# Fewer chunks of 384 tokens, more of 512, and three transforms packed more closely

## The chip, the cores and the metric

One core of one Trainium2 chip. The metric is the device time of one execution in microseconds (us), the median of several runs.

## The reference

The input x has 4 batches of 3008 positions with 256 channels. Per batch: a real Fourier transform along the positions, a complex 256x256 mix with biases, a soft threshold of 0.01 on real and imaginary parts, and the inverse transform. The 12032 resulting rows ("tokens") then go through a two-layer network with 2048 hidden units and a leaky activation whose slope is learned per unit:

```python
X = np.fft.rfft(x, axis=1); Xr, Xi = X.real, X.imag
Yr = Xr @ w_r - Xi @ w_i + b_r
Yi = Xr @ w_i + Xi @ w_r + b_i
Yr = np.sign(Yr) * np.maximum(np.abs(Yr) - lam, 0.0)      # Yi likewise
y = np.fft.irfft(Yr + 1j * Yi, n=x.shape[1], axis=1).reshape(-1, 256)
h = y @ w_in
out = (np.maximum(h, 0.0) + alpha * np.minimum(h, 0.0)) @ w_out
```

## The kernel before

**The transform** of a batch is four stages of matrix products, 3008 being 47 x 64. Stage a works on 16 row groups (`a_split`, `a_mm`, `a_evac`) and stores its result to a DRAM tile `ad`. Stage b reads that back in another order, in 12 pairs (`b_load`, `b_mm`, `b_evac`, `b_evac2`). On each pair the complex mix follows with three real products (`m_mm` two, `m_mm2` the third), the threshold in eight parts (`m_part`, lines 520 to 538), and stage c (`c_mm`, `c_evac`), stored to a DRAM tile `zd`. Stage d reads `zd` in 8 blocks of 376 tokens a batch; it is the "last stage" and yields tokens as columns, split into a high and a low float32r part (`d_load`, `d_mm`, `d_part`, `d_step`; in the wide part `s_dmm`, `s_dpart`). So in each batch all of a comes before the first pair of b, and all of c before the first block of d, through DRAM.

**The network, classic part.** Tokens 0 to T0 are cut into CC chunks of 384 (the first of a run of 16 has 256). One step is one chunk and one of 16 tiles of 128 hidden units. `l1_step` makes six matmuls of up to 384 columns into PSUM (three products of high and low parts, two halves of the channels), ACT takes the relu of the negated sum (line 686), DVE adds it scaled (687), ACT makes the high part gh (691), and DVE or POOL in turn the low part gl (692). `l2_step` makes nine matmuls of 256 columns for the step three behind. At the end of a chunk the third accumulator goes out through the tile `ot`, the other two through `os`.

**The network, wide part.** From T0 on, chunks of 512 tokens, in pairs of hidden tiles, PR = 8 pairs a chunk (`s_l1`, `s_sums`, `s_l2`): twelve matmuls of 512 columns, then seven block products in place of eight (21 matmuls of 256 columns instead of 24), with sums and differences of blocks on ACT, DVE and POOL. Pair 1 of each chunk takes the eight plain products. The last chunk has 384 tokens and is classic in its products. `s_out` and `s_turn` combine and transpose the result.

**The order** is written out by hand in program order; each engine and each DMA queue executes its instructions in that order and waits on semaphores. `at(i, fn, ...)` files work under classic step i. In a step, `l1_step` runs first, with the work of `mid` (parts of the mix) inside it; then the stores collected before are issued on SP's queue (`put`), then `l2_step`, then the work of `todo`. Batch 0 is transformed before the classic part begins. Of batch b + 1, row group g of stage a stands at step AO[b+1] + 3g/2 (its split two steps earlier, its load of x five steps before), and pair q at a step i: `b_load` at i - 4, `b_mm` to `b_evac2` at i, `m_mm` at i + 2, the mix's third product and parts at i + 3 to i + 6, `c_mm` and `c_evac` at i + 8. Batch 1's row groups are done by step 15. The first 48 steps run the first J = 3 chunks side by side, while the network's weights are taken apart (`pump`). Blocks of the last stage stand three steps ahead of their chunk (61, 77, 93, 109, ...). The 26 last classic steps prepare the weights of the wide part (`w_open`, `w_full`, `w_sums`, `w_split`), in the buffers of the transforms' tables, and its first blocks. In the wide part `pre` and `post` file the blocks of the last stage under pairs.

**Buffers that the change touches in time.** `ps_f` is a PSUM pool of three buffers for the outputs of stages a, b, the mix, c and d in program order; `ps_h` has two for L1. `ot` (line 722) and `sm`, the sum of stage b (line 453), share one buffer. `zst` (two buffers) holds the outputs of c and, in batches 2 and 3, of a, until their stores have landed. `xt` (two) holds loads of x, `bt` (three) those of stage b. `Xh` and `Xl` (two each) hold a pair from i to i + 4.

Of the kernel before, what the change touches and what calls it, by code (L numbers as in the profile page):

```python
# [93 lines left out]
def fft_mix_moe(ctx, tc, x, w_r, w_i, b_r, b_i, w_in, w_out, alpha, la, rb, lc, rd, lf, cf, sel, out):  # L94
# [12 lines left out]
    TC = 384  # L107
    assert NC * TC - 128 == NC * TOK

    CC = 16  # L110
    SC = 512

    def head(c):
        return 128 - (TC - TOK) * (c % NC) if c % NC else 0

    def size(c):
        return TC if c % NC else TC - 128

    T0 = (CC // NC) * NC * TOK + TC * (CC % NC) - (128 if CC % NC else 0)
    NS2 = -(-(B * S - T0) // SC)  # L120
# [12 lines left out]
    def f(t):  # L133
        return t.bitcast(F32)
# [443 lines left out]
    def d_open(c):  # L578
# [3 lines left out]
        if head(c):  # L582
            for t, src in zip((hi, lo), heads.pop(c)):
                if c < CC:
                    t, src = t[:, :, 0:head(c)], f(src)[:, :, 0:head(c)]
# [8 lines left out]
    def d_step(b, g):  # L594
        t = zt.pop((b, g))
        c = NCH * b + g
        assert c < CC
        n0 = (size(c) - head(c)) // CH
# [20 lines left out]
    def s_open(n):  # L619
        yt[CC + n] = [work.tile([128, CT, SC], F32R, tag=tag, name=tag) for tag in ("yh", "yl")]  # L620

    def s_parts(dg):

        s, e = TOK * dg, TOK * dg + TOK
        for n in range(max(s - T0, 0) // SC, (e - 1 - T0) // SC + 1):
            a, z = max(s, T0 + SC * n), min(e, T0 + SC * (n + 1))
            yield n, (a - s) // CH, (z - s) // CH, a - T0 - SC * n, z - T0 - SC * n
# [7 lines left out]
    def s_dpart(dg, n):  # L635
        parts = []
        for k, n0, n1, a, z in s_parts(dg):
            if k == n:
                for ct in range(CT):
                    ps = ds[dg][ct][:, :, n0:n1]  # L640
                    ys = [y[:, ct] for y in yt[CC + n]]
                    if n == NS2 - 1:
# [92 lines left out]
    PR = FT // 2  # L735
# [39 lines left out]
    def s_l1(n, t):  # L775
        yh, yl = yt[CC + n]
        w1 = SC if n < NS2 - 1 else ZC
        q = work.tile([128, 2, SC], F32, tag="xt", name="sq")[:, :, 0:w1]
        for j in range(2):
            m = 2 * t + j  # L780
            ps = ps_h.tile([128, SC], F32, tag="h", name="ps_h")[:, 0:w1]
            k = 0
            for ct in range(CT):
                for w, a in ((0, yh), (0, yl), (1, yh)):
                    PE.matmul(ps, wi_h[m // FH][:, w, ct, 128 * (m % FH):128 * (m % FH) + 128], a[:, ct, 0:w1],  # L785
                              start=(k == 0), stop=(k == 3 * CT - 1))
                    k += 1
            A.activation(out=q[:, j], in_=ps, func=AF.Relu, scale=-1.0)  # L788
            V.scalar_tensor_tensor(out=q[:, j], in0=q[:, j], scalar=beta_s[:, m:m + 1], in1=ps,  # L789
                                   op0=ALU.mult, op1=ALU.add)  # L790
        sq[n, t] = q
# [160 lines left out]
    ES = [1, 1, 1, 1, 1, 1, 1, 1, 1, 0, 1, 0, 0, 0, 0, 0]  # L952
    LOS = [0, 1, 0, 0, 1, 1, 0, 1, 1, 0, 1, 1, 0, 1, 0, 0, 1, 1, 0, 0, 1, 0, 1, 1, 1, 1, 1, 0, 1, 1, 0, 1, 1, 0, 1, 1, 0, 1, 1, 0, 1, 1, 0, 1, 1, 0, 1, 1]
    DS = 3
    AO = {2: 92, 3: 146}
    BO = {2: 126, 3: 176}
    BP = 4
    SLAG = 2
    PLAIN = (1,)
    MP = [3, 4, 4, 4, 4, 5, 5, 6]  # L960
    CM = 8
    PB = 49
    BL = 4
    LM = 26
    MM, M2 = 2, 4
# [17 lines left out]
    with tc.manual_schedule():  # L983
# [100 lines left out]
        def at(i, fn, *args, when=todo):  # L1084
            when.setdefault(i, []).append((fn, args))
# [9 lines left out]
        for b in range(B):  # L1095
            s0 = b * per
            for g in range(J if b == 0 else 0, min(NCH, CC - NCH * b)):
                i = s0 + g * FT
                at(i - 8, d_load, b, g)
                at(i - 4 if i == J * FT else i - FT + 1, d_open, NCH * b + g)  # L1100
                if b == 0 and g == J:
                    at(i - DS, d_step, b, g)
                else:
                    at(i - 3, d_step, b, g)
            if b == 0:
                for g in range(FILL, NG):
                    i = 6 * (g - FILL) + 9
                    if g % 2 == 0:
                        at(i - 8, a_load, 1, g // 2)
                    at(i, a_mm, 1, g)  # L1110
                    at(i, a_evac, 1, g)
            else:
                for g in range(NG if b + 1 < B else 0):
                    i = AO[b + 1] + 3 * g // 2
                    if g % 2 == 0:
                        at(i - 5, a_load, b + 1, g // 2)
                    at(i - 2, a_split, b + 1, g)
                    at(i, a_mm, b + 1, g)
                    at(i, a_evac, b + 1, g)
            for q in range(NPAIR if b + 1 < B else 0):  # L1120
                i = PB + 11 * q // 2 if b == 0 else BO[b + 1] + BP * q
                at(i - BL, b_load, b + 1, q)
                at(i, b_mm, b + 1, q)
                at(i, b_evac, b + 1, q)
                at(i, b_evac2, b + 1, q)
                at(i + MM, m_mm, b + 1, q)
                at(i + M2, m_mm2, b + 1, q, when=mid)
                for n, k in enumerate(MP):
                    at(i + k, m_part, b + 1, q, n, when=mid)
                at(i + MP[6], m_evac1, b + 1, q)  # L1130
                at(i + CM, c_mm, b + 1, q)
                at(i + CM, c_evac, b + 1, q)
# [3 lines left out]
        pre, post = {}, {}  # L1136
        i = NS - 26
        at(i, w_open)
        for p in range(PR // 2):
# [3 lines left out]
            for k in range(2):  # L1143
                at(i + 6 * p + 3 + k, w_split, p, k, False)
                at(i + 6 * p + 4 + k, w_split, p, k, True)
        at(NS - 14, d_open, CC)
        for dg in range(CC, B * NCH):
            ns = [n for n, *_ in s_parts(dg)]
            first = PR * (ns[-1] - 1) - 1
            if len(ns) == 2:  # L1150
                at(first, s_dmm, dg, when=pre)
                at(first, s_dpart, dg, ns[0], when=pre)
                at(first, s_open, ns[1], when=post)
                at(first, s_dpart, dg, ns[1], when=post)
            elif dg > CC:
                first += 6
                at(first, s_dmm, dg, when=pre)
                at(first, s_dpart, dg, ns[0], when=pre)
            else:
                first = -6  # L1160
                at(NS - 6, s_dmm, dg)
                at(NS - 6, s_dpart, dg, ns[0])
            if first < 0:
                at(NS + first - 5, d_load, dg // NCH, dg % NCH)
            else:
                at(first - 3, d_load, dg // NCH, dg % NCH, when=pre)
# [25 lines left out]
        for k in range(len(spairs) + SLAG):  # L1192
# [9 lines left out]
            if k >= SLAG:  # L1202
                n, t = spairs[k - SLAG]
# [43 lines left out]
```

## Time and profile before

| | us |
|---|---|
| runs, three | 1369.5, 1369.52, 1370.37; median 1369.52 |
| the profiled execution | 1370.45 |
| its span, first to last instruction | 1368.7 |

The profile's page gives, for each engine, its busy time and share of the span: PE is TensorE's matmuls, PEld its weight loads, DVE VectorE, ACT ScalarE, POOL GpSimd; SP is the engine that issues most DMAs.

| engine | busy share |
|---|---|
| PE | 99% |
| PEld | 93% |
| DVE | 73% |
| ACT | 55% |
| POOL | 29% |

A matmul's end is modelled and matmuls overlap, so its start, and the distance to the next start, say more than its duration. In the profile the first matmul of a classic step starts at 108.4 us, the first of the wide part at 836.5 us. A timeline row is: start, duration, engine, line, operation, output<-input, shapes, count, and in brackets the idle time of the engine ahead of it with what ended it.

### The profile page before, as it was taken

The page shows a single profiled execution, that of the slowest core. Times are in us where ns is not written, and L with a number is a line of the kernel's source. Part 1 is how long each engine was busy: PE and PEld are TensorE (multiplying, and loading weights), DVE is VectorE, ACT ScalarE, POOL GpSimd, SP SyncE. Part 2 cuts the span into 40 slices and gives each one's busy share as a digit, 9 for nine tenths or more (in the row PEclk, how much of TensorE's full clock was granted, in tenths as well). Part 3 has the DMA queues.
Part 4 walks back from the last instruction along what each step waited for, and adds up shares of the span by engine and source line. Part 5 has one row for each costly group of instructions (what it writes and reads, how often), then busy time and mean ns, then how long its engine had stood idle before and what let it go on. Part 6 is the DMA issues. An engine that isn't in the chain of part 4 may idle for free.

```text
span 1368.7 us, 25199 instructions
## 1 busy us (share of the span) xinstructions
PE 1352.7 (99%) x9367; PEld 1274.7 (93%) x9367; DVE 993.1 (73%) x1821; ACT 749.5 (55%) x1528; POOL 400.1 (29%) x421
## 2 busy tenths in 40 slices
PE   8999999999999999999999999999999999999998
PEld 5979899999999999899999999999999999999998
DVE  2767855666665677676777667788888888888885
ACT  3566555445565455554545555555565556555653
POOL 3864832222222322223323221211121211211222
PEclk9999999999999999999999999999999999999999
DMA  9965222113332124321211111010011101110001
GB/s 234 258 175 151 78 93 67 50 36 85 120 92 74 47 85 127 95 72 62 65 45 58 44 36 36 12 28 16 13 40 28 26 5 37 29 28 7 22 17 28
DMA packets 82903, 89.66 MB, mean 66 GB/s; under 512 B 35567, under 2 KB 65234, under 8 KB 82781
## 3 DMA queue, kind: packets, MB, share of 16 engines
q1 hardware_dynamic: 74214, 76.76, 19.4%
q0 software_dynamic: 5168, 8.02, 2.2%
q10 hardware_dynamic: 3399, 3.27, 0.7%
q8 instruction: 74, 1.21, 0.4%
q14 instruction: 48, 0.39, 0.1%
HBM read 50.49 MB, written 34.34 MB: 62 GB/s over the span
## 4 chain that ended last, share of the span: by engine, by line
PE 92%; DVE 3%; ACT 2%; issue 1%; DMA 1%; POOL 0%; ACTq 0%; SPq 0%; DVEq 0%; POOLq 0%
PE ps_h L785 19%; PE ps_h L680 17%; PE ps_m L486 5%; PE ps_o L887 4%; PE ps_o L888 4%; PE ps_o L886 4%; PE ps_o L719 4%; PE ps_o L718 4%; PE ps_o L717 4%; PE ps_d L611 4%; PE ps_b L426 3%; PE ps_m L473 3%; PE o_last L719 2%; PE o_last L717 2%; PE o_last L718 2%; PE ps_a L387 2%
## 5 line engine op out<-in xcount | busy, mean ns | idle before, releaser
L680 PE MATMUL ps_h<-yh,w 128*128 128x384 f32 (+1 forms) x960 | 282.8, 336 | 1.6 <-DVE q L687 1.5
L785 PE MATMUL ps_h<-yh,w 128*128 128x512 f32 (+1 forms) x768 | 251.7, 388 | 0.0
L687 DVE SCALAR_TENSOR_TENSOR q<-q,beta_s,ps_h 128x384 f32<-128x384 f32 (+1 forms) x256 | 154.5, 604 | 123.1 <-ACT q L686 122.0
L691 ACT ACTIVATE gh<-q 128x384 fp32r<-128x384 f32 (+1 forms) x256 | 132.8, 519 | 186.2 <-DVE q L687 181.9
L692 POOL TENSOR_TENSOR gl<-q,gh 128x384 fp32r<-128x384 f32 (+1 forms) x123 | 132.1, 1075 | 349.1 <-ACT gh L691 326.8
L824 POOL TENSOR_TENSOR l<-t,h 128x512 fp32r<-128x512 f32 x77 | 99.9, 1297 | 389.8 <-ACT h L822 357.6
L680 PEld LDWEIGHTS ps_h<-yh,w 128*128 128x128 f32 x960 | 176.7, 189 | 4.8 <-issue 1.3
L785 PEld LDWEIGHTS ps_h<-yh,w 128*128 128x128 f32 x768 | 143.9, 188 | 26.1
L789 DVE SCALAR_TENSOR_TENSOR sq<-sq,beta_s,ps_h 128x512 f32<-128x512 f32 (+1 forms) x192 | 133.9, 731 | 44.3 <-ACT sq L788 43.4
L680 PE MATMUL ps_h<-yl,w 128*128 128x384 f32 (+1 forms) x480 | 159.2, 332 | 0.0
L785 PE MATMUL ps_h<-yl,w 128*128 128x512 f32 (+1 forms) x384 | 148.6, 387 | 0.0
L719 PE MATMUL ps_o<-w,gl 128*128 128x256 f32 x512 | 144.5, 282 | 3.3 <-POOL gl L692 3.3
L686 ACT ACTIVATE q<-ps_h 128x384 f32<-128x384 f32 (+1 forms) x256 | 122.0, 477 | 45.3 <-PE ps_h L680 41.3
L718 PE MATMUL ps_o<-w,gh 128*128 128x256 f32 x512 | 144.6, 282 | 0.0
L717 PE MATMUL ps_o<-w,gh 128*128 128x256 f32 x512 | 144.1, 282 | 0.0
L804 ACT ACTIVATE dh<-sq 128x768 fp32r<-128x768 f32 x88 | 74.5, 846 | 92.4 <-DVE sq L789 61.3
L788 ACT ACTIVATE sq<-ps_h 128x512 f32<-128x512 f32 (+1 forms) x192 | 106.3, 585 | 23.2 <-PE ps_h L785 22.4
L692 DVE TENSOR_TENSOR gl<-q,gh 128x384 fp32r<-128x384 f32 (+1 forms) x133 | 80.1, 602 | 30.5 <-ACT gh L691 28.5
L719 PEld LDWEIGHTS ps_o<-w,gl 128*128 128x128 f32 x512 | 97.4, 190 | 4.1 <-POOL gl L692 3.9
L718 PEld LDWEIGHTS ps_o<-w,gh 128*128 128x128 f32 x512 | 97.3, 190 | 0.1
L717 PEld LDWEIGHTS ps_o<-w,gh 128*128 128x128 f32 x512 | 96.5, 188 | 0.1
L822 ACT ACTIVATE h<-t 128x512 fp32r<-128x512 f32 x77 | 48.7, 633 | 82.1 <-DVE t L820 79.9
(211 smaller groups left out, 3471.9 us busy)
## 6 DMA issues: line engine op xcount, KB each, us to landing
zt<-zd SPq DMA_DIRECT2D x32, 384.0 KB
ad<-ast SPq DMA_DIRECT2D x48, 192.0 KB
bt<-ad SPq DMA_DIRECT2D x72, 128.0 KB
zd<-zst SPq DMA_DIRECT2D x36, 256.0 KB
xt<-in_x SPq DMA_DIRECT2D x21, 320.0 KB
cw_s<-in_moe_w_in SPq DMA_DIRECT2D x8, 512.0 KB
cw_s<-in_moe_w_out SPq DMA_DIRECT2D x8, 512.0 KB
out<-oT SPq DMA_DIRECT2D x120, 32.0 KB
```

Of the source, the lines that this page charges most:

```text
L680: PE.matmul(ps, wi_h[m // FH][:, w, ct, 128 * (m % FH):128 * (m % FH) + 128], a[:, ct, 0:n], start=(k == 0), stop=(k == 3 * CT - 1))
L686: A.activation(out=q, in_=ps, func=AF.Relu, scale=-1.0)
L687: V.scalar_tensor_tensor(out=q, in0=q, scalar=beta_s[:, m:m + 1], in1=ps, op0=ALU.mult, op1=ALU.add)
L691: A.activation(out=hi, in_=q, func=AF.Copy)
L692: (V if LOS[(2 * m + c) % len(LOS)] and fill or not fill and (m + c) % 2 else G).tensor_tensor(out=lo, in0=q, in1=f(hi), op=ALU.subtract)
L717: PE.matmul(a, hi[:, t], w[:, 0], start=(i, k) in first, stop=False)
L718: PE.matmul(a, hi[:, t], w[:, 1], start=False, stop=False)
L719: PE.matmul(a, lo[:, t], w[:, 0], start=False, stop=(i, k) in last)
L785: PE.matmul(ps, wi_h[m // FH][:, w, ct, 128 * (m % FH):128 * (m % FH) + 128], a[:, ct, 0:w1], start=(k == 0), stop=(k == 3 * CT - 1))
L788: A.activation(out=q[:, j], in_=ps, func=AF.Relu, scale=-1.0)
L789: V.scalar_tensor_tensor(out=q[:, j], in0=q[:, j], scalar=beta_s[:, m:m + 1], in1=ps, op0=ALU.mult, op1=ALU.add)
L824: G.tensor_tensor(out=l24, in0=t24, in1=f(h24), op=ALU.subtract)
```

## The change

CC, the number of classic chunks, goes from 16 to 12, so T0 goes from 6016 to 12 x 384 - 128 = 4480 and the number of wide chunks (NS2) from 12 to 15, the last with 384 tokens in both. Classic steps go from 256 to 192. The pairs of the transforms of batches 1, 2 and 3 stand every 3 steps (batch 1 had every 5.5, batches 2 and 3 every 4), at 49 to 82, 86 to 119 and 123 to 156; they stood at 49 to 109, 126 to 170 and 176 to 220. The row groups of batches 2 and 3 stand at 58 to 80 and 95 to 117; they stood at 92 to 114 and 146 to 168. `s_open`, which reserves the buffers of a wide chunk, is filed for every chunk, not only where a block reaches across two chunks.

```diff
-    CC = 16
+    CC = 12
...
-    AO = {2: 92, 3: 146}
-    BO = {2: 126, 3: 176}
-    BP = 4
+    AO = {2: 58, 3: 95}
+    BO = {1: 49, 2: 86, 3: 123}
+    BP = 3
...
-    PB = 49
...
-                i = PB + 11 * q // 2 if b == 0 else BO[b + 1] + BP * q
+                i = BO[b + 1] + BP * q
...
+        for n in range(1, NS2):
+            at(PR * (n - 1) - 1, s_open, n, when=post)
...
                 at(first, s_dpart, dg, ns[0], when=pre)
-                at(first, s_open, ns[1], when=post)
                 at(first, s_dpart, dg, ns[1], when=post)
```

## Rows read from the trace of the kernel before

**Rows 1.** The page, busy us (share of the span) and instructions.
```profile
PE 1352.7 (99%) x9367; PEld 1274.7 (93%) x9367; DVE 993.1 (73%) x1821; ACT 749.5 (55%) x1528; POOL 400.1 (29%) x421
```

**Rows 2.** The page, chain that ended last, shares by engine.
```profile
PE 92%; DVE 3%; ACT 2%; issue 1%; DMA 1%; POOL 0%; ACTq 0%; SPq 0%; DVEq 0%; POOLq 0%
```

**Rows 3.** Windows: six bare classic steps; four with a pair; four with row groups too.
```profile
core 0: us, PE busy (x) PEld busy (x) DVE busy (x) ACT busy (x) POOL busy (x), PEclk, DMA share, GB/s
423.90:436.62 12.72, 12.72 (x93) 12.72 (x91) 5.36 (x10) 6.11 (x12) 3.06 (x3) 1.00 0.33 105
684.36:696.57 12.21, 12.21 (x95) 12.21 (x94) 8.80 (x17) 6.06 (x12) 3.30 (x5) 1.00 0.18 59
516.48:530.80 14.32, 14.32 (x102) 13.79 (x101) 9.96 (x20) 8.49 (x18) 4.03 (x4) 1.00 0.42 125
```

**Rows 4.** Windows: wide chunks with one and two blocks; a classic step with a block.
```profile
856.37:900.39 44.02, 44.02 (x284) 40.09 (x284) 36.49 (x66) 25.74 (x49) 9.09 (x7) 1.00 0.03 10
900.39:946.22 45.83, 45.83 (x300) 41.88 (x300) 39.34 (x78) 26.46 (x55) 9.08 (x7) 1.00 0.09 21
436.62:440.45 3.83, 3.83 (x34) 3.83 (x32) 1.67 (x4) 1.98 (x4) 0.70 (x1) 1.00 0.01 3
```

**Rows 5.** Chain in order of time: start, us; L1 of a classic step, of a pair.
```profile
424.06 1.04 PE ps_h L680 x6
...
861.59 2.75 PE ps_h L785 x12
```

**Rows 6.** Groups by line and form: count, busy us, mean ns, idle before.
```profile
L692 POOL TENSOR_TENSOR gl<-q,gh 128x384 fp32r<-128x384 f32 x116 | 126.4, 1089 | 341.2 <-ACT gh L691 318.9 <-PE ps_b L426 8.0 <-PE ps_h L680 7.4
L692 DVE TENSOR_TENSOR gl<-q,gh 128x384 fp32r<-128x384 f32 x124 | 74.6, 602 | 27.4 <-ACT gh L691 25.6 <-PE ps_h L680 1.2
...
L446 DVE TENSOR_TENSOR Xl<-ps_b,Xh 128x512 fp32r<-128x512 f32 x48 | 33.1, 689 | 32.9 <-ACT Xh L440 32.7
L509 DVE TENSOR_TENSOR Yt<-Yt,Yc 128x512 f32<-128x512 f32 x36 | 32.0, 889 | 1.2
L440 ACT ACTIVATE Xh<-ps_b 128x512 fp32r<-128x512 f32 x48 | 28.5, 594 | 20.1 <-PE ps_b L426 20.1
L404 ACT ACTIVATE ast<-ps_a 96x512 f32<-96x512 f32 x48 | 27.6, 584 | 7.9 <-PE ps_a L387 4.8 <-DMA zd<-zst 2.0 <-DMA ad<-ast 0.8
L518 DVE TENSOR_TENSOR Yl<-Yt,Yh 128x512 fp32r<-128x512 f32 x36 | 24.8, 690 | 0.0
L142 DVE TENSOR_TENSOR xl<-xt,xh 94x512 fp32r<-94x512 f32 x32 | 23.4, 733 | 19.7 <-ACT xh L139 16.2 <-DMA xt<-in_x 1.7 <-DMA bt<-ad 0.6
L139 ACT ACTIVATE xh<-xt 94x512 fp32r<-94x512 f32 x32 | 19.8, 618 | 0.0
L456 DVE TENSOR_TENSOR sm<-ps_b,sm 128x256 f32<-128x256 f32 x36 | 15.3, 424 | 22.1 <-ACT sm L455 22.1
```

**Rows 7.** Windows, columns as in rows 3: three stretches of the third one's make-up.
```profile
501.25:516.48 15.23, 14.55 (x104) 13.82 (x102) 11.57 (x21) 8.97 (x19) 4.56 (x6) 1.00 0.31 95
546.16:561.05 14.89, 14.65 (x103) 13.90 (x103) 10.48 (x20) 8.50 (x20) 4.94 (x6) 1.00 0.29 87
561.05:577.21 16.16, 15.75 (x102) 13.63 (x101) 9.25 (x19) 7.68 (x16) 3.21 (x5) 1.00 0.30 90
```

**Rows 8.** Timeline of ACT: the copy of L455 behind a store of ot.
```profile
363.15 0.39 ACT L455 ACTIVATE sm<-ps_b 128x256 f32<-128x256 f32 x1 [0.85 <-DMA out<-ot]
...
570.76 0.39 ACT L455 ACTIVATE sm<-ps_b 128x256 f32<-128x256 f32 x1 [4.46 <-DMA out<-ot]
```

**Rows 9.** Timeline of SP: issues of stores of ot and of loads.
```profile
360.94 0.61 SPq L334 DMA_DIRECT2D out<-ot  x1
...
563.22 1.10 SPq L418 DMA_DIRECT2D bt<-ad  x2
564.41 0.88 SPq L358 DMA_DIRECT2D xt<-in_x  x2
565.38 0.62 SPq L334 DMA_DIRECT2D out<-ot  x1
```

## The prediction, made blind

> **What bounds the kernel now.** I read first the busy times of the engines, then the chain that ended last, then the lengths of single stretches. TensorE is busy for 1352.7 of 1368.7 us [rows 1], and 92% of the chain that ended last is TensorE [rows 2]. A busy TensorE need not be one at its peak, since matmuls overlap, so the lengths of stretches decide. A window row gives the stretch, its length, and the busy time of TensorE, its weight loads, VectorE (DVE), ScalarE (ACT) and GpSimd (POOL), then the granted clock, the DMA share and GB/s. Six classic steps with nothing beside them take 12.72 us, 2.12 us each; a stretch of four steps with one pair of a transform takes 12.21 us, and one of four steps with a pair and three row groups of the next batch's first stage 14.32 us [rows 3]. In all three TensorE is busy throughout, at a granted clock of 1.00, the 2.4 GHz level, and DVE for only 5.36, 8.80 and 9.96 us. So where these patterns run undisturbed, the time is the sum of TensorE's work: a pair costs it 12.21 - 4 x 2.12 = 3.73 us, a row group (14.32 - 12.21) / 3 = 0.70 us. An edit is worth what it changes in that sum, less what new waits give back.
>
> **The change part by part.**
> CC = 12: chunks 12 to 15, 1536 tokens, leave the classic part. This removes 4 x 16 = 64 classic steps and adds three wide chunks of 512 tokens, 24 wide pairs; 64 x 384 and 24 x 2 x 512 are the same 24576 token-tiles, so no work is lost or doubled. Removed: 64 x 2.12 = 135.7 us. A wide chunk with one last-stage block in it takes 44.02 us, one with two 45.83 us [rows 4]; a block is 1.81 us, a wide chunk alone 42.21 us. Added: 3 x 42.21 = 126.6 us. Net: -9.1 us.
> Last-stage blocks: all 32 stay; four of them move from classic steps to wide chunks. In a classic step a block costs 3.83 - 2.12 = 1.71 us [rows 4] against 1.81 us, so the bound is 0 to +0.4 us. I take 0, because the classic step after a block also starts a little late, which the 1.71 leaves out.
> The saving in rows: a classic step has six matmuls of 384 columns in 1.04 us, 173 ns each, and nine of 256 in the remaining 1.08 us, 120 ns each; a wide pair has twelve of 512 columns in 2.75 us, 229 ns each [rows 5], and 21 of 256 instead of the 24 that its tokens would need. The Trainium skill (TensorE: Matmul & The Clock Gate, Back-to-back issue gap) puts the warm gap at N / 2.4 + 2.5 ns, thus 162.5, 109 and 216 ns; an estimate from that page is 1.96 us a classic step and 39.4 us a wide chunk, so 125.3 - 118.2 = 7.1 us saved in place of 9.1. The measured spacings are 11 to 13 ns above that gap in every width, so I keep the rows.
> BP = 3, BO, AO: the 36 pairs of the three later transforms and the 32 row groups keep every instruction, so TensorE's sum is unchanged; they now share fewer classic steps (49 to 164, where they had 49 to 228). Per pair TensorE needs 3 x 2.12 + 3.73 = 10.09 us; DVE needs 8.80 less one step's 5.36 / 6 = 0.89, 7.91 us (78%), ACT 6.06 - 1.02 = 5.04 us [rows 3]. Where batch 2's and batch 3's row groups run too (8 pairs each, two groups a pair), TensorE needs 11.50 us, DVE 7.91 + 2 x 0.73 = 9.37 us (81%), ACT 5.04 + 2 x (0.62 + 0.58) = 7.44 us [rows 3, 6]. No engine passes TensorE, so the sum holds if the order of the work doesn't stall it.
> PSUM: the pool ps_f has three buffers and gets six tiles a pair in the order b, a, p1, a, c, m. The tightest is the second a, which takes b's buffer. TensorE reaches it after one a, one L1 part, m_mm2 (about 0.71 us, six matmuls of 256) and one L2 part, 0.70 + 1.04 + 0.71 + 1.08 = 3.5 us after b. The buffer is free after the ACT copy, the DVE difference and the DVE sum, 0.59 + 0.69 + 0.42 = 1.7 us, or 2.3 us with a gl of 0.60 in front [rows 6]. That leaves 1.2 us, so cost 0; if DVE runs later than that, every microsecond beyond is lost on TensorE. On the other hand one step no longer carries p1, c, b and a together, as every fourth one does now.
> Stalls: three stretches with the same make-up as the 14.32 us one take 15.23, 14.89 and 16.16 us [rows 7], which is 0.91 + 0.57 + 1.84 = 3.3 us lost. The first has the first row group after the crowded step, the second follows a last-stage block. The third is a wait of ACT: the copy of L455 waits 4.46 us for the store of ot, since sm and ot share one buffer [rows 8]; that store was issued at 565.38 behind a load of x at 564.41 and landed at about 570.7, 5.3 us later, where another, issued at 360.94, held the same copy to 363.15, 2.2 us, and cost little [rows 8, 9]. After the change ot is written at steps 66, 82, ..., 162, and a pair's sm in the same step at 82 and 98, one step later at 67 and 147; before, in the same step at 82, 98, 130, 146 and 162. So there are two hits instead of five, and four last-stage blocks among the row groups (61, 77, 93, 109). For the new stalls I take 4 x 0.57 + 2 x 0.5 = 3.3 us (a hit nearer to the 2.2 us landing than to the 5.3), between 0 (every one hidden) and 4 x 1.84 + 4 x 0.91 = 11 us. With 3.3 gone and 3.3 new, nothing changes.
> SP's queue: the first b_load of a batch now stands two steps behind the last store of its row groups (step 82 behind 80, 119 behind 117), where it stood 8 and 4 behind. SP waits there, and the stores of ot, os and zst wait behind it. A store takes 2.2 to 5.3 us; the load is issued in 1.10 us [rows 9], and I bound its flight by the 5.3 of the slow store. Sum at most 11.7 us; the first b_mm comes six steps behind the last row group, 12.7 us even of bare steps. Cost 0, and up to 5 us for each of two batches if that cover goes. The later pairs' loads keep their lead of four steps.
> POOL, DVE, d_open: s_open only reserves buffers, now also for wide chunk 3, which begins where batch 2 begins. d_open(12) copies a head of 32 tokens on POOL, two instructions that other idle time covers. w_open keeps its place, two steps behind the last c_mm (166 behind 164, as 230 behind 228). All 0.
>
> **Sum.** The profiled execution took 1370.45 us, with a span of 1368.7; the median of the runs is 1369.52, 0.07% less. -9.1 + 0 - 3.3 + 3.3 gives 1361.3 for the profiled one, 1360.4 us against the median. About 0.2% (2.7 us) is what a measurement of this kernel can tell from no change.
>
> **The rivals.**
> More waits on the ot store and on the last-stage blocks, the upper bound above: 1369.5 - 9.1 - 3.3 + 11 = 1368.1, in the middle 1364.3. For it: the 16.16 us stretch. Against: four of the five hits now cost 0.9 us or less. Chance 0.14, most of it still faster by more than 0.2%.
> Handshakes use up the tighter spacing: each pair is 0.2 us longer than TensorE's sum (as the same DVE form varies between 0.69 and 0.89 us [rows 6]), 36 x 0.2 = 7.2 us, total 1369.5 - 9.1 + 7.2 = 1367.6, no change to be measured. Against: the 12.21 us stretch shows no idle TensorE at all. Chance 0.10.
> DVE is blocked by POOL (the other side). Five or six DVE instructions of a pair with row groups read two SBUF tiles; a POOL gl takes 1.09 us [rows 6]. If each waited half a gl, 0.55 us, DVE would need 9.37 + 5.5 x 0.55 = 12.4 us where TensorE needs 11.50: 0.9 us on each of 16 pairs is 14.4 us, and the result 1369.5 - 9.1 + 14.4 = 1374.8, slower. It decides from a mean wait of (11.50 - 9.37 + 0.74) / 5.5 = 0.52 us, where 16 x 0.74 = 11.8 us turn the gain into 2.7 us lost. For it: L509 takes 0.89 us where L518, of the same form, takes 0.69; against it: that is 0.2 us, L518 shows nothing, and the means already hold the present share of it. Chance 0.10. The Trainium skill (SBUF — State Buffer, SBUF: two separate sides) has the rule behind this: a DVE instruction with two SBUF inputs and a GpSimd one that reads SBUF take one port in turn, the later waiting for all of the other. By that rule the wait could reach a whole gl; the trace agrees with a mean of 0.2 us in one line only.
> That the change doesn't do what it says: only its 9.1 us are at stake, as the token-tiles match; part of the 0.10 above.
>
> **How the numbers follow.** The forecast, 1357 (no stalls left: 1369.5 - 9.1 - 3.3 = 1357.1) to 1363.5, has 0.66. The first rival has 0.14, the second 0.10, the third 0.10. The range 1357.0 to 1367.6 holds the forecast, the first rival's middle and half of the second; it leaves out the third and the ends. Faster by over 0.2%: 0.66 + 0.14 = 0.80; within: 0.10; slower: 0.10.
>
> **What would show it right or wrong.** The classic part should end some 136 us less far behind, the wide chunks should take 44.0 or 45.8 us as before, and a pair should take 10.1 us without and 11.5 us with row groups, TensorE busy throughout. Wrong would be: pairs longer than that with TensorE waiting for DVE q L687 or for the release of a ps_f tile; L455 waiting for out<-ot by several us; b_mm idle on bt<-ad at the start of batch 2 or 3; POOL and DVE instructions longer than now in the dense part.

## The result, and the profile after

The changed kernel takes 1357.67 us (median of four runs, 1356.33 to 1358.56), the kernel before beside it 1369.94 (1369.5 to 1370.55): a ratio of 0.9909, with a 95% interval of 0.9892 to 0.9926. It is 12.3 us faster; 1360.4 was forecast, within 1357.0 to 1367.6. The profiled execution took 1358.56 us, its span is 1356.8.

The page of the kernel after, busy times and the shares of the chain that ended last:

```profile
PE 1341.8 (99%) x9208; PEld 1253.9 (92%) x9208; DVE 1036.9 (76%) x1930; ACT 760.7 (56%) x1528; POOL 382.7 (28%) x404
...
PE 92%; DVE 2%; DMA 2%; ACT 1%; issue 1%; POOL 0%; ACTq 0%; SPq 0%; DVEq 0%; POOLq 0%
```

TensorE still sets the end, with 10.9 us less to do than in [rows 1]. Where the time went is read from two starts. The first L1 matmul of step 48, where the change begins to act, comes at 209.20 us in both kernels. The first L785 matmul, where the wide part begins, comes at 836.52 before and at 690.75 after. So the classic part lost 627.3 - 481.5 = 145.8 us, and the wide part, to the end of the span, grew from 532.1 to 666.0, by 133.9: together -11.9 us.

Windows of the kernel after, columns as in rows 3: the first three wide chunks; four pairs with row groups (12 steps); one pair without (3 steps); two single steps.

```profile
690.75:733.15 42.40, 42.40 (x271) 38.40 (x270) 33.34 (x62) 25.68 (x52) 8.79 (x7) 1.00 0.11 29
733.15:777.17 44.02, 44.02 (x286) 40.10 (x285) 38.23 (x71) 25.41 (x48) 9.08 (x7) 1.00 0.13 31
777.17:823.00 45.83, 45.83 (x301) 41.88 (x300) 39.01 (x77) 26.84 (x55) 9.09 (x7) 1.00 0.09 21
...
264.38:310.42 46.04, 46.04 (x334) 44.59 (x333) 35.38 (x66) 29.00 (x59) 12.57 (x17) 1.00 0.44 132
539.05:549.14 10.09, 10.09 (x79) 10.09 (x78) 7.31 (x14) 4.62 (x11) 2.71 (x4) 1.00 0.16 54
433.14:439.95 6.81, 6.30 (x50) 6.12 (x49) 5.20 (x12) 4.06 (x11) 1.01 (x1) 1.00 0.42 124
394.78:398.27 3.49, 3.40 (x22) 3.02 (x21) 1.53 (x3) 1.35 (x4) 1.02 (x3) 1.00 0.13 42
```

The wide chunks with one and two blocks take what they took before [rows 4]. The first, 42.40 us, has one block too; it is shorter because its first pair (3.84 us) runs beside the second layer of the last classic steps and not yet beside that of a pair, and the first wide chunk of the kernel before took the same 42.40. No full chunk is without a block, but the length of one follows from single pairs: seven of 5.23 us and the plain one of 5.62 make 42.23, where 42.21 was inferred. A pair with row groups takes 46.04 / 4 = 11.51 us, one without 10.09 us, with TensorE busy throughout: the closer spacing costs TensorE nothing. Of these windows only the last two lose time. Step 109 (6.81 us) holds a block of the last stage, c and m at once. A step with c and m takes 4.28 us in this kernel, and a block adds 1.80 (step 173, with nothing else beside it, takes 3.83 us and the one behind it 2.21, where bare steps take 2.12), so 0.73 us are lost. Step 99 (3.49 us) follows a store of `ot`; the same 22 records take 3.17 us in a run below that removes this wait, so 0.32 us are lost. Together that is 1.05 us.

Their waits, in the trace after: TensorE's waits by what they wait for (us, times, longest), that one wait of step 109 (m waits until DVE, on line 142, has taken `hl`, part of the block's low half, out of the block's PSUM tile), and the summary of ACT's copy L455 between 330 and 410 us.

```profile
PE ps_m L486 <- DVE hl L142: 0.5, 1, 0.5
```

```profile
438.46 0.71 PE L486 MATMUL ps_m<-ws_s,Xh 128*128 128x256 f32 x4 [0.51 <-DVE hl L142]
```

```profile
its engine sat idle before it (us, times) until:
  DVE Xl L446: 4.7, 5
  DMA out<-ot: 4.1, 2
```

Two copies wait for a store of `ot`, 4.1 us in sum, where five did before (two of them in [rows 8]). No matmul of stage b waits for its load `bt<-ad`.

Groups by line and form, after, to be read beside [rows 6]:

```profile
L692 POOL TENSOR_TENSOR gl<-q,gh 128x384 fp32r<-128x384 f32 x84 | 92.6, 1102 | 258.8 <-ACT gh L691 245.6 <-PE ps_m L486 6.7 <-PE ps_h L680 4.1
...
L692 DVE TENSOR_TENSOR gl<-q,gh 128x384 fp32r<-128x384 f32 x92 | 55.7, 605 | 18.3 <-ACT gh L691 16.6 <-PE ps_h L680 1.2
...
L509 DVE TENSOR_TENSOR Yt<-Yt,Yc 128x512 f32<-128x512 f32 x36 | 25.8, 716 | 1.2
L518 DVE TENSOR_TENSOR Yl<-Yt,Yh 128x512 fp32r<-128x512 f32 x36 | 24.6, 684 | 0.0
```

The means of DVE's two-input forms are not longer in the denser part. L509, the only one that had looked long, went from 889 to 716 ns; what its mean hides is told with the rivals below.

### The profile page after: what moved, and what is told of

The parts are those of the page before. It is cut to its first block, busy times and chain, and to the rows that moved or that the text cites. A ratio compares the mean times of both kernels' runs of the same rounds, so it can differ in the third digit from the quotient of the medians.

```text
span 1356.8 us, 25103 instructions
## 1 busy us (share of the span) xinstructions
PE 1341.8 (99%) x9208; PEld 1253.9 (92%) x9208; DVE 1036.9 (76%) x1930; ACT 760.7 (56%) x1528; POOL 382.7 (28%) x404
## 4 chain that ended last, share of the span: by engine, by line
PE 92%; DVE 2%; DMA 2%; ACT 1%; issue 1%; POOL 0%; ACTq 0%; SPq 0%; DVEq 0%; POOLq 0%
PE ps_h L785 24%; PE ps_h L680 13%; PE ps_m L486 6%; PE ps_o L887 6%; PE ps_o L888 6%; PE ps_o L886 6%; PE ps_d L611 4%; PE ps_o L719 3%; PE ps_o L718 3%; PE ps_o L717 3%; PE ps_b L426 3%; PE ps_a L387 2%; PE o_last L719 1%; PE o_last L717 1%; PE o_last L718 1%; PE o_last L886 1%
## 5 line engine op out<-in xcount | busy, mean ns | idle before, releaser
L785 PE MATMUL ps_h<-yh,w 128*128 128x512 f32 (+1 forms) x960 | 315.6, 389 | 0.0
L785 PEld LDWEIGHTS ps_h<-yh,w 128*128 128x128 f32 x960 | 180.0, 188 | 33.2
L680 PE MATMUL ps_h<-yh,w 128*128 128x384 f32 (+1 forms) x704 | 206.0, 335 | 1.3 <-DVE q L687 1.2
L785 PE MATMUL ps_h<-yl,w 128*128 128x512 f32 (+1 forms) x480 | 186.3, 388 | 0.0
L687 DVE SCALAR_TENSOR_TENSOR q<-q,beta_s,ps_h 128x384 f32<-128x384 f32 (+1 forms) x192 | 115.5, 601 | 81.8 <-ACT q L686 80.2
L680 PE MATMUL ps_h<-yl,w 128*128 128x384 f32 (+1 forms) x352 | 116.4, 331 | 0.0
L718 PE MATMUL ps_o<-w,gh 128*128 128x256 f32 x384 | 108.4, 282 | 0.0
L717 PE MATMUL ps_o<-w,gh 128*128 128x256 f32 x384 | 108.1, 282 | 0.0
L785 PEld LDWEIGHTS ps_h<-yl,w 128*128 128x128 f32 x480 | 90.5, 189 | 13.6
L819 DVE TENSOR_TENSOR dl<-sq,dh 128x768 fp32r<-128x768 f32 x98 | 93.4, 953 | 3.7 <-ACT dh L804 3.6
L888 PE MATMUL ps_o<-l,sw_a 128*128 128x256 f32 x294 | 82.0, 279 | 0.0
L886 PE MATMUL ps_o<-h,sw_a 128*128 128x256 f32 x294 | 81.9, 279 | 0.0
```

Of the source, the lines that this page charges most:

```text
L687: V.scalar_tensor_tensor(out=q, in0=q, scalar=beta_s[:, m:m + 1], in1=ps, op0=ALU.mult, op1=ALU.add)
L717: PE.matmul(a, hi[:, t], w[:, 0], start=(i, k) in first, stop=False)
L718: PE.matmul(a, hi[:, t], w[:, 1], start=False, stop=False)
L886: PE.matmul(o, wh, gh, start=first, stop=False)
L888: PE.matmul(o, wh, gl, start=False, stop=last)
```

## The experiments

Ratios and differences are against the kernel that each batch of runs had beside it (1370.05, 1370.1, 1370.02 and 1370.22 us, the kernel before). "Classic part" is the time between the two starts above: 627.3 us before, 481.5 after.

**The packing alone.** The change with CC left at 16.

```diff
-    CC = 12
+    CC = 16
```

> The packing alone: the new steps of pairs and row groups, but CC = 16, so all 256 classic steps stay. Theory (TensorE's sum plus named stalls): no matmul is added or removed, so only the waits change. The 3.3 us that the kernel before loses in three stretches go, and about 1.1 us come (a block that meets c and m in step 109, and the ot store in step 98), as in the changed kernel: 1369.9 - 2.2 = 1367.7 us, ratio 0.998. Rival (the packing is what makes the kernel faster): near 1358 to 1360 us, ratio 0.992. Second rival (the packing costs, and CC hides it): above 1370 us.

Measured: 1367.67 us (11 runs), 0.9986 [0.9978, 0.9995]. The classic part takes 624.4 us, 2.9 less than before; the wide part keeps its 532.1. The same two steps stall as in the full change. So the closer spacing is worth about 2.4 us and the moved chunks the other ten. (The chunks alone, with the old places of the pairs, make no kernel: the last c stood at step 228, and 12 chunks have 192 steps.)

**One more plain pair in each wide chunk.** Pair 2 also takes eight block products instead of seven; nothing is left out, the result is the same by a longer way.

```diff
-    PLAIN = (1,)
+    PLAIN = (1, 2)
```

> The changed kernel with a second plain pair in every wide chunk (eight products in place of seven in pair 2 too). Theory (a wide chunk is cheaper than classic steps because of the seventh-for-eighth product): each of the 14 full wide chunks gets 3 matmuls of 256 columns at 0.12 to 0.13 us more, 5.0 to 5.5 us in all, 1357.7 + 5.3 = 1363 us; the plain pair then takes 5.6 us and the other 5.2. Rival (the gain comes from the 512 columns of the first layer, or the vector engines bound the wide part): under 1 us more, or even less time, since the plain pair has fewer sums.

Measured: 1363.66 us (5 runs), 0.9952 [0.9939, 0.9964], 6.0 above the changed kernel. Windows of this run, the first three wide chunks:

```profile
690.44:733.24 42.80, 42.80 (x274) 38.78 (x272) 31.80 (x59) 24.81 (x51) 7.49 (x6) 1.00 0.10 29
733.24:777.63 44.39, 44.39 (x288) 40.48 (x287) 37.00 (x68) 24.93 (x47) 7.79 (x6) 1.00 0.12 30
777.63:823.84 46.21, 46.21 (x305) 42.28 (x303) 37.64 (x74) 26.28 (x54) 7.79 (x6) 1.00 0.08 21
```

Each is 0.37 to 0.40 us longer, although DVE has 1.2 to 1.5 us less to do. In the wide part a product of TensorE is paid for in full, and work of DVE is not. At 0.38 us a pair, the seven shortened pairs of each of the three added chunks save 7 x 0.38 x 3 = 8.0 of the 9.1 us that the forecast's sum gives; no run tells the other 1.1 apart.

**A buffer of its own for `sm`, in the kernel before.**

```diff
-            sm = work.tile([128, 256], F32, tag="ot", name="sm", bufs=1)
+            sm = work.tile([128, 256], F32, tag="sm", name="sm", bufs=1)
```

> The kernel before with a buffer of its own for sm, so that it no longer waits for the store of ot. Theory (the shared buffer costs the 1.84 us of the third stretch): that stretch falls from 16.16 to about 14.3 us, the other two stay at 15.2 and 14.9, the whole at 1369.9 - 1.8 = 1368.1 us. Rival (the crowded step with p1, c, b and a is what stalls): the stretch stays at 16 us and the time at 1369.9.

Measured: 1368.64 us (11 runs), 0.999 [0.9981, 0.9999]; the classic part takes 625.3 us, 2.0 less. The stretch that took 16.16 us [rows 7] is back at its sum:

```profile
559.93:574.38 14.45, 14.45 (x102) 13.82 (x101) 10.33 (x20) 9.07 (x19) 4.22 (x6) 1.00 0.37 109
```

The other two stretches of rows 7 take 15.23 and 14.89 us as before. So the shared buffer cost this stretch 1.7 of its 1.84 us and the step behind it another 0.2, and the other two nothing.

**Both stalls of the changed kernel taken away:** the buffer as above, and block 7 of batch 0 a step earlier, out of the step with c and m.

```diff
-                    at(i - 3, d_step, b, g)
+                    at(i - 4 if (b, g) == (0, 7) else i - 3, d_step, b, g)
```

> The changed kernel with a buffer of its own for sm, and the last-stage block of batch 0's last chunk one step earlier, in step 108 instead of 109, so that it no longer meets c and m. Theory (these two are all that the changed kernel still loses to the packing): the 0.27 us of step 99 and the 0.8 us of step 109 go, 1357.7 - 1.1 = 1356.6 us. Rival (the loss in 109 is the block's own and moves with it): step 108 loses 0.5 to 0.8 us, the whole 1357.4 us.

Measured: 1357.41 us (4 runs), 0.9909 [0.9895, 0.9922]. Windows: step 99, then steps 108 and 109:

```profile
394.26:397.43 3.17, 3.17 (x22) 2.98 (x21) 2.06 (x5) 1.67 (x5) 1.54 (x3) 1.00 0.29 90
428.77:434.29 5.52, 5.50 (x41) 5.18 (x40) 4.21 (x10) 2.65 (x8) 2.14 (x3) 1.00 0.39 108
434.29:438.56 4.27, 4.27 (x34) 4.26 (x33) 3.07 (x8) 2.82 (x7) 0.00 (x0) 1.00 0.21 53
```

Step 99 is 0.32 us shorter, and steps 108 and 109 together 0.55 (9.79 us, where the change takes 3.53 + 6.81). The classic part is 0.9 us shorter than the change's; the times of the two kernels can't tell that apart. Step 108 keeps a little: a step of the same make-up, 77, takes 5.36 us in the change.

**c in the same step as b and a** (its place nine steps behind b), which loads one step of three with three stages.

```diff
-    CM = 8
+    CM = 9
```

> The changed kernel with c_mm and c_evac one step later (i + 9), so that c, b and the first row group of a period meet in one step, as they did in the crowded step of the kernel before. Theory (only a wait that TensorE meets counts, and three PSUM buffers with the new order still have over 1 us to spare): the period stays at 11.5 us with row groups and 10.1 us without, the total at 1357.7 us within 0.7. Rival (spreading the stages over the three steps of a period is what took the stalls away): each of the 16 periods with row groups loses 0.5 to 0.9 us as the stretches at 501 and 546 us did, 8 to 14 us, 1366 to 1372 us.

Measured: 1366.76 us (9 runs), 0.9978 [0.9968, 0.9988], 9 above the changed kernel; the classic part is 9.7 longer. The step that lost most, 125, with its clock, and a steady period of three steps:

```profile
497.47:506.10 8.63, 7.27 (x51) 7.09 (x50) 5.46 (x11) 3.90 (x10) 2.33 (x3) 0.87 0.06 18
288.13:299.77 11.64, 11.64 (x86) 11.21 (x85) 9.10 (x18) 6.95 (x14) 2.35 (x4) 1.00 0.48 143
```

```profile
PE ps_a L390 <- ACT zst L561: 3.5, 5, 1.0
```

Where nothing else lands on the crowded step, a period is only 0.13 us longer than 11.51. The loss is in eight steps, 0.4 to 2.7 us each, among them those with a block (61, 125, 141), with the first row group of a batch (58, 95) or just behind a store of `ot` (67). The wait that grew is that of a's matmul for ACT's copy of c. The rival's total came true, but not its account: it had every period with row groups lose 0.5 to 0.9 us.

**Pairs every two steps,** the change's spacing taken one further.

```diff
-    AO = {2: 58, 3: 95}
-    BO = {1: 49, 2: 86, 3: 123}
-    BP = 3
+    AO = {2: 50, 3: 79}
+    BO = {1: 49, 2: 78, 3: 107}
+    BP = 2
```

> The changed kernel with pairs every 2 classic steps instead of 3 (batches at 49, 78 and 107, row groups at 50 and 79); 28 more classic steps are then bare. Theory (TensorE's sum): a pair needs TensorE for 2 x 2.12 + 3.73 = 7.97 us and DVE for 8.80 - 2 x 0.89 = 7.02 us (88%), with 1.33 row groups 8.9 against 8.0 us, so nothing changes: 1357.7 us within 1. Rival (the handshakes between DVE and ACT, or DVE blocked by POOL, use up the spacing): DVE idles while TensorE waits, a pair takes 8.5 to 9 us, 36 x 0.5 to 1.0 is 18 us or more, 1376 us. What lies between is told by the length of the pairs.

Measured: 1390.7 us (4 runs), 1.015 [1.0136, 1.0164], 33 above the changed kernel. The offsets 2, 4 and 8 are all even, so m, the third product, c and b meet in every second step. Windows: a pair with a row group, a pair without; and the waits that grew:

```profile
276.21:286.26 10.05, 9.50 (x67) 8.71 (x65) 7.90 (x15) 5.45 (x12) 3.46 (x5) 1.00 0.36 102
524.59:532.90 8.31, 8.25 (x64) 8.04 (x63) 7.09 (x14) 3.91 (x9) 2.26 (x3) 1.00 0.35 108
```

```profile
PE ps_b L426 <- ACT zst L561: 6.7, 11, 1.0
PE ps_a L390 <- DVE Yt L530: 4.0, 13, 0.9
PE ps_c L554 <- DVE Yt L530: 3.5, 2, 1.9
```

By the forecast's sum a bare pair is 2 x 2.12 + 3.73 = 7.97 us; it takes 8.31, with DVE busy for 7.09 of it. A pair with one row group would be 8.67 and takes 10.05. Here the handshakes that the forecast feared do cost.

**The same with the offsets spread,** c at seven steps and the third product at three, so that no two fall together.

```diff
-    CM = 8
+    CM = 7
-    MM, M2 = 2, 4
+    MM, M2 = 2, 3
```

> Pairs every 2 steps as in the run that took 1390.7 us, but m_mm2 at i + 3 and c_mm at i + 7, so that b and m stand in even steps and the third product and c in odd ones, where all four stood in even steps. Theory (what costs is several stages of the transform in one step, not the spacing): a pair without row groups falls from 8.3 us to TensorE's 8.0, one with row groups from 10.4 to about 9.0, and the whole from 1390.7 to under 1365 us. Rival (DVE or the handshakes cannot keep a pair per two steps): the pairs stay as long as they are, 1385 us or more.

Measured: 1402.26 us (4 runs), 1.0236 [1.0223, 1.025], 11.6 worse than without the spread. Crowding of steps was therefore not the whole cause. The same two lines, put on the kernel before with its wide spacing:

> The kernel before with m_mm2 at i + 3 and c_mm at i + 7: with pairs every 4 steps the third product, c, b and a row group then no longer share a step; b stands alone, m two steps on, the third product and c in the step after. Theory (crowding makes the stalls of the stretches at 501 and 546 us): 0.91 and 0.57 us go; of the 1.84 us behind the ot store some stays, since the shared buffer stays: 1370.0 - 1.5 = 1368.5 us or, with all three gone, 1366.7. Rival (the first row group and the blocks stall wherever they stand): no change, 1370 us.

Measured: 1392.96 us (4 runs), 1.0167 [1.0154, 1.0181], and the classic part 19.7 us longer, although pairs there have four steps. Then c's offset alone, on the kernel before:

> The kernel before with the product c seven steps after b instead of eight, and the third product left where it was (four steps after b); its companion moved both and came to 1392.96 us, 22.9 over the kernel before, with the classic part 19.7 longer. Theory (a product must stand clear of the copies of the result that it reads: c reads what the second eviction of b's chain leaves in the two halves of the split, and at seven steps it stands one step behind it): moving c alone costs most of the 22.9, so 1383 to 1391 us, with waits of c's third matmul for the lower half of the split as in the companion, some 4 us and more in sum, and the classic part 640 us or longer. Rival (the loss came from the third product beside m, which take the same three buffers): moving c alone costs little, 1369 to 1375 us, with the classic part under 632 us.

Measured: 1380.75 us (4 runs), 1.0082 [1.0065, 1.0099], the classic part 636.9 us. That lies between the two expectations: c alone costs 10.5 us, the third product moved as well the other 12.4. Waits of both runs (c alone first):

```profile
PE ps_c L556 <- DVE Yl L518: 4.2, 5, 1.7
```

```profile
PE ps_c L556 <- DVE Yl L518: 4.1, 6, 1.0
PE ps_a L390 <- DVE Yc L524: 3.7, 3, 1.7
```

The longest of them in the run of c alone, on TensorE and on DVE:

```profile
584.63 0.39 PE L556 MATMUL ps_c<-Yl,lc_s 128*128 128x256 f32 x1 [1.72 <-DVE Yl L518]
```

```profile
582.51 0.69 DVE L142 TENSOR_TENSOR xl<-xt,xh 94x512 fp32r<-94x512 f32 x1 [0.75 <-ACT xh L139]
583.36 0.61 DVE L687 SCALAR_TENSOR_TENSOR q<-q,beta_s,ps_h 128x384 f32<-128x384 f32 x1 [0.17 <-ACT q L686]
583.89 0.68 DVE L518 TENSOR_TENSOR Yl<-Yt,Yh 128x512 fp32r<-128x512 f32 x1
```

c's third matmul needs Yl. On DVE's queue Yl stands behind the split of a row group, which itself waits for ACT, and behind a q. At eight steps this delay is covered by a whole step, at seven it falls on TensorE. With the third product moved too, the matmul of a waits for Yc, what DVE makes of m's PSUM tile. These waits show the mechanism and not the whole size: the 4.2 us stand beside 9.5 by which the classic part grew with c alone.

**The pairs' loads one step ahead** instead of four.

```diff
-    BL = 4
+    BL = 1
```

> The changed kernel with each load of stage b one step ahead of its pair instead of four. Theory (the loads have cover to spare: SP runs ahead of TensorE, and is held only by the last store): a load is issued some 6 us ahead of its matmuls and takes 2.2 to 5.3 us, no change, 1357.7 us within 0.7. Rival (the loads are what the closer packing nearly lacks time for): b_mm waits for bt<-ad in most pairs, 36 x 0.5 us or more, 1376 us.

Measured: 1398.2 us (4 runs), 1.0206 [1.0191, 1.0221], 40 above the changed kernel. The waits, then one load on SP and the matmul that waits for it:

```profile
PE ps_b L426 <- DMA bt<-ad: 25.2, 24, 4.1
```

```profile
295.48 0.99 SPq L358 DMA_DIRECT2D xt<-in_x  x2
296.56 0.32 SPq L334 DMA_DIRECT2D ad<-ast  x1
296.97 1.20 SPq L418 DMA_DIRECT2D bt<-ad  x2
```

```profile
303.26 0.68 PE L426 MATMUL ps_b<-rb_s,bt 128*128 128x128 f32 x4 [2.07 <-DMA bt<-ad]
```

Behind a load of x, the load is used 6.3 us after its issue. Four steps cover that (three take 10.1 us), one step does not.

**Still fewer classic chunks:** CC = 10, with pairs every two steps and row groups every 4/3 steps (`AO` 50 and 77, `BO` 49, 76 and 102).

> Pairs every 2 steps, row groups every 1.33 steps, and CC = 10: 32 more classic steps go (67.8 us), two full wide chunks come (84.4 us) and the last chunk falls from 384 to 128 tokens (from 8 x 4.23 us to 8 x about 1.55 us if its matmuls bound it, 21.4 us less). Theory (TensorE's sum): -67.8 + 84.4 - 21.4 = -4.8 us, 1352.9 us. Rival (the transforms no longer fit beside so few classic steps, DVE or the handshakes bind): no gain or a loss, 1358 us or more. Second rival (the last chunk of 128 tokens is bound by its evictions): it takes over 2.3 us a pair, which gives 6 us back, 1359 us.

Measured: 1406.01 us (4 runs), 1.0269 [1.0252, 1.0286], 48 above the changed kernel. The transforms stall as in the two runs above with that spacing (stage b waits for ACT's copy of c 13 times, 7.7 us). The clock is also down at the end, where the last wide chunk has only 128 tokens: 25 us at a mean granted clock of 0.66.

```profile
1380.00:1405.00 25.00, 23.74 (x138) 23.53 (x137) 10.94 (x33) 8.72 (x30) 3.24 (x7) 0.66 0.09 22
```

**A version meant to beat both:** CC = 11, `sm` apart, the block moved, batches 1 and 2 every three steps and batch 3 every two, the offsets spread.

> A version meant to beat both: CC = 11, one more full wide chunk and a last chunk of 256 tokens, sm with a buffer of its own, the block of batch 0 one step earlier, m_mm2 at i + 3 and c_mm at i + 7, pairs of batches 1 and 2 every 3 steps and of batch 3, which has no row groups beside it, every 2. Theory (TensorE's sum, kept free of stalls by spreading): 16 classic steps less (33.9 us), a wide chunk more (42.2 us), the last chunk 8 x 2.83 instead of 8 x 4.23 us (11.2 us less), so -2.9 us, and -0.9 for the two named stalls: 1357.7 - 3.8 = 1353.9 us. Rival (pairs every 2 steps cost batch 3 what they cost before, some 0.35 to 1.3 us a pair): 4 to 16 us back, 1358 to 1370 us.

Measured: 1375.32 us (9 runs), 1.0035 [1.0021, 1.0048]: slower than both. The loss is in the classic part, 468.1 us where the forecast's terms ask for 446.8 (481.5 less 33.9 and 0.9). It shows the waits of the spread offsets again; they are those of row groups, so they stand in the batches with a pair every three steps:

```profile
PE ps_a L390 <- DVE Yc L524: 9.1, 12, 1.9
```

CC = 11 with the old offsets was not tried.

## Why the prediction was right, and where it was off

**The sum of TensorE's work** was the right bound. The forecast's terms give -135.7 for the classic steps and -4 x 1.80 = -7.2 for the blocks that leave them (1.80 us each as above, where the prediction had bounds of 1.71 and 1.81), -142.9 in all; the classic part lost 145.8. In the wide part they give 126.6 + 4 x 1.81 = 133.8; it grew by 133.9. The -9.1 us is thus shown by the windows, and the cause of 8.0 of it, the product left out in the pairs of the wide chunks, by the run with one more plain pair.

**Packing at no cost** held: 11.51 and 10.09 us a pair, where 11.50 and 10.09 were forecast. It held for these offsets, and the reason given was incomplete, so that it held was in part luck. The PSUM argument named one tight reuse, the second a taking b's buffer, with 1.2 us to spare. No a waited there in any run; waits for b's buffer (line 456) come to 1.9 us at most, in the run of CC = 10. The runs that lost time waited above all for the copy of c, for what DVE makes of the mix's PSUM tiles (Yc, Yt) and for Yl, places for which the prediction had worked out no slack. At three steps a pair and offsets of 2, 4 and 8 all of them have enough; every step more or less at a place that was tried, on the change (c, the spacing of the pairs) or on the kernel before (c, the third product), cost 9 to 33 us.

**The old stalls, -3.3 us,** went, and they were a little more: the classic part lost 2.9 us more than its sum asks, with the 1.05 us of new stalls already taken off, so about 4.0 us of old ones went. The three stretches of the forecast hold 3.3. Of the rest, 0.4 us stood in step 93 of the kernel before, with a block, b and a row group; here it is, and behind it step 61 of the change, with the same make-up:

```profile
338.18:344.11 5.93, 5.74 (x43) 5.39 (x42) 3.83 (x9) 3.63 (x10) 1.00 (x1) 1.00 0.35 98
251.03:256.57 5.54, 5.54 (x44) 5.36 (x43) 3.94 (x9) 3.24 (x9) 1.00 (x1) 1.00 0.24 84
```

The 1.84 us were the shared buffer, as the run with a buffer of its own shows.

**The new stalls are the step that was over-sized.** 3.3 us were taken for them; the trace has 1.05, 0.73 in step 109 and 0.32 in step 99 (the expectations above say 0.8 and 0.27). Of the two hits of `ot`, foreseen at steps 82 and 98, the first cost nothing; of the four blocks only the one that meets c and m in one step lost time, and the one at 93 has no row group beside it. "4 x 0.57" gave every block the loss of one stretch, without asking which steps a block shares. That is 2.2 us, and with the 0.7 of old stalls that the forecast hadn't counted it makes up, within 0.1, the 2.8 by which the spans differ from the sum (-11.9 against -9.1).

**SP's queue at no cost** held: the trace after has no wait of a stage b for its load. The forecast had a load take 1.10 us to issue and at most 5.3 in flight, 6.4 in all; the run with one step's lead shows 6.3 us from issue to use behind a load of x.

**The rivals.** More stalls: two were found, not eight. Handshakes: not in the change, but they are what a spacing of two meets. DVE blocked by POOL: it asked for a mean wait of 0.52 us on each two-input DVE instruction of the dense part, and that did not come: L518 has 684 ns after and 690 before, L509 fell to 716. But the prediction's reading, a mean of 0.2 us in one line, hides two lengths. In the kernel before, 17 of the 36 L509 take 1.10 to 1.12 us and 19 take 0.69. Each of the 17 starts while POOL's L458 (the low part of `sm`) is running and ends 0.55 us after it; none of the 19 starts beside a running POOL instruction. One of the 17, and one of the run with pairs every two steps, where L509 starts just behind a gl; DVE's row stands above POOL's:

```profile
641.49 1.11 DVE L509 TENSOR_TENSOR Yt<-Yt,Yc 128x512 f32<-128x512 f32 x1
641.12 0.93 POOL L458 TENSOR_TENSOR Xl<-sm,Xh 128x256 fp32r<-128x256 f32 x1
```

```profile
297.21 1.54 DVE L509 TENSOR_TENSOR Yt<-Yt,Yc 128x512 f32<-128x512 f32 x1
297.19 1.01 POOL L692 TENSOR_TENSOR gl<-q,gh 128x384 fp32r<-128x384 f32 x1 [0.30 <-ACT gh L691]
```

By the rule of the Trainium skill (SBUF — State Buffer, SBUF: two separate sides) such waits could reach a whole gl of 1.1 us; the trace agrees, with about 0.42 us behind L458 and, with pairs every two steps, 0.80 to 0.85 behind a gl. So the rival's mechanism is real, and what it had wrong is how often the two meet: 17 of 36 times in the kernel before, 2 of 36 in the change and with the packing alone, 19 with pairs every two steps. The means follow (889, 716, 715 and 970 ns), and in sum L509 waited 7.1 us before and 0.8 after. Whether any of these waits reached TensorE was not traced.

## What to carry to other kernels

When one engine is busy throughout, price a rearrangement by that engine's sum from bare windows, and then ask of each stage that is moved how far it stands behind the result or the buffer that it needs, with everything queued before that result on the other engines. An even spread of stages over the steps is no aim by itself: here two spread versions lost more than the crowded one, and the waits of the one with the wide spacing name a stage that came too close to its producer. Size a stall only for the steps in which it meets other work, not for every repeat of it. And where the mean of a form looks long, look at its single instances: a mean can be a mix of two lengths, and what the long ones meet tells the cause.

## What the runs showed of the hardware

A loss of time on TensorE can cost twice. In the kernel before with the two spread offsets, step 149 takes 7.46 us with TensorE busy for 4.71 of them, and in the next step the granted clock is down:

```profile
521.92:529.38 7.46, 4.71 (x33) 4.14 (x32) 4.64 (x8) 4.92 (x10) 2.14 (x2) 1.00 0.31 104
529.38:534.63 5.25, 5.25 (x28) 5.06 (x26) 2.76 (x6) 2.11 (x4) 0.14 (x1) 0.67 0.55 164
```

A step with the same stages, in the changed kernel, at the full clock:

```profile
439.95:443.65 3.70, 3.70 (x28) 3.54 (x27) 2.51 (x4) 2.21 (x5) 0.68 (x1) 1.00 0.20 71
```

The same 28 matmul records take 5.25 us at a mean clock of 0.67, a mix of the 2.4 and 1.2 GHz levels, and 3.70 us at 1.00: the waits of step 149 cost 1.55 us more in the step behind them. The same is seen where the pairs' loads come late (a granted clock of 0.58 between 228 and 236 us). So the waits that a trace names can cost more than their sum. Between step 48 and the wide part the changed kernel shows no such stretch: TensorE is busy for 480.96 of 481.55 us at a granted clock of 1.00.

DVE's L509, whose two inputs are both in SBUF, waits for a POOL instruction that is already running. In every run it takes 0.69 us when none is running at its start; when L458 or a gl is, it ends 0.54 to 0.56 us after that instruction does, whatever the POOL instruction still had to do. L446, which has the same 128x512 elements but one input in PSUM, takes 0.68 to 0.69 us in the changed kernel in all 15 cases of the classic part in which it starts beside a running gl.
